# Seven stacked passes for the rest rows of the contraction, with their weights built ahead

## The chip, the cores and the metric

The kernel runs on one core of one Trainium2 chip. The metric is the device time of one execution in microseconds (us). The core has a matrix engine (PE, which loads a stationary tile of up to 128 x 128 and streams columns against it), a vector engine (DVE), a scalar engine (ACT), a general engine (POOL), and a queue (SP) from which this kernel issues all its DMAs. Each engine and the queue work off their own instructions strictly in the order of the program and wait for each other by semaphores.

## The reference

```
x  = A_x                                    # 1 x 2048 x 576
xn = layernorm(x)
out = x + A(xn) + B(xn)

A: qkv = xn @ wqkv                          # 576 x 1728, 32 heads of 18
   each token attends to 8 earlier tokens, 2 apart (0, 2, ..., 14 back), masked below token 0
   softmax over the 8, weighted sum of v, then @ wo           # 576 x 576
B: h = xn @ w1 + b1                         # 576 x 4608
   mish(h) = h * tanh(softplus(h)), then @ w2                 # 4608 x 576
```

All inputs and the output are fp32.

## The kernel before

**Number format.** A product of two fp32 matrices is made of three passes on PE in a rounded fp32 format: each operand is split into a high part (a cast, done by ACT) and a low part (what is left, a subtraction on DVE or POOL), and high x high, low x high and high x low are summed in PSUM.

**Halves, blocks, tiles.** The 2048 tokens are two halves (`hf`) of 1024. A half has two blocks (`b`) of 512 tokens, a block four tiles (`jj`) of 128. `ln_norm` or `norm1` normalises a tile, `ln_transpose` and `transpose_split` transpose it on PE and split it into the operand `XTs[hf, b]`.

**Seven products for eight.** The first 512 rows of the contraction and the 1024 tokens are cut in 2 x 2 blocks, the weights likewise, and a Strassen-Winograd scheme is used: with A11, A12, A21, A22 the token blocks by rows of the contraction, and B11 to B22 the weights (two feature tiles of F1, or two groups of QKV), the operands S1 to S4 and T1 to T4 are sums of them, and seven products (A11 B11, A12 B21, S1 T1, S2 T2, S3 T3, S4 B22, A22 T4) replace eight. A product of 256 rows is six passes (`prod`, line 986; in the QKV groups `za_part`, line 702). S is made once for a half (`s_step`, `s_high`, `s_low`, lines 943 to 981, the sums on POOL). T is made for each pair of F1 by `w1_sums` (POOL) and for the QKV groups by `za_sum` (DVE).

**The rest rows.** 576 = 512 + 64. The last 64 rows of the weights are held twice in a tile of 128 partitions, and the operand has the high part of the 64 rows above and the low part below. Two passes (`rest`, line 1000) with the weights' high and low part make a full product. The rest is not part of the seven products: four of them (A12 B21, S1 T1, A22 T4, S4 B22) get a rest product added, with the rest of block 0 or 1 or their difference (`rem`), so that the four outputs are whole. The rest weights are part of the tiles of F1's weights (`wa` is 5 x 128 wide, `wc` 3 x 128) and two units of their own (R2, R3) of a QKV group pair.

**The stages.** Half 0: the QKV groups 0 and 1 directly (`qkv_item`, 14 passes a tile, four tiles a block), the groups 2 and 3 by seven products ("y"), then 18 pairs `q` of F1's feature tiles (`m1_part`, parts 0 to 5), each followed by the second layer F2 for the pair before (`m2_pair`). The weights are loaded, split on ACT and DVE (`make`, `low`) and stored in DRAM in both parts (`keep`). Half 1: transposes between the last items of F2, then the groups 0 and 1 ("v") and 2 and 3 ("z") by seven products, then the 18 pairs with the kept weights (`fetch`), F2 by seven products for six pairs of pairs (`p_item`), and last the product with wo (`wo_part`). Attention runs beside F1: POOL multiplies, DVE sums; it reads k and v through four `kv` tiles (`load_kv`).

**The order.** `plan` is a list of items, each a piece of work on PE in that place, with background work that is issued just before it. `before(i, ...)` puts a load, a sum, a split or a store at item i; a table `MOVED` shifts some of them. Items 0 to 3 are group 0 of block 0 of half 0; 4 to 6 and 8 group 1 of block 0; 7, 9, 11 and 13 the transposes of the four tiles of block 1; 10, 12, 14 and 15 group 0 of block 1; 16 to 19 group 1 of block 1; "y" begins at item 20, attention's first step is at item 26. The raw weights of "y" are loaded at items 8 to 12 (`za_load`). PSUM has four banks with the tag `h` and four with the tag `out`; a transposed tile takes two of `h`, a QKV item one.

The steps of the prediction touch `transpose_split` (lines 317 to 339), `ln_norm` (440), `ln_transpose` (449), `qkv_item` (610), `first_item` (1543), `prod` and `rest` (986, 1000), `m1_part` (1057), `za_part` (702), `attention` (837) and the places in `plan` from line 1663 on.

## Time and profile before

| what | value |
|---|---|
| runs (3) | 1089.81, 1089.99, 1090.22 us, median 1089.99 |
| span of the profiled execution, first to last instruction | 1088.0 us (its own device time is not listed; the median run is 1.99 us longer than this span) |
| PE busy | 1081.0 us, 6454 matmuls |
| weight loads of PE | 997.7 us |
| DVE busy | 892.9 us, 1475 instructions |
| ACT busy | 513.6 us, 946 |
| POOL busy | 787.4 us, 630 |
| DMA | 283.99 MB, mean 261 GB/s |

The profile is of one execution. A row of the groups by line gives the line, the engine, the operation, the output and inputs by the program's names with their shapes, the count, then the busy time of the group and the mean of one instruction in ns, then the idle time ahead of them and who ended it. The chain of waits follows the work that ended last back to the start; its rows are start, length, engine and line. Matmuls overlap in the pipeline, so the length of one in the groups is more than what it adds to a row of them.

### The profile page before, as it was taken

To read this page: it belongs to the slowest core of one execution; us is meant where nothing else is said; L and a number is where in the kernel's file an instruction comes from. 1 tells how busy PE (TensorE), PEld (TensorE's weight loads), DVE (VectorE), ACT (ScalarE), POOL (GpSimd) and SP (SyncE) were. 2 spreads that over 40 slices of the span, in tenths; PEclk is the share of its full clock that TensorE was granted. 3 is DMA by queue.
4 is the path that set the end of the run, shared out by engine and by line. 5 is a ranking of instruction groups with operands and counts; after the bars stand their busy time and mean duration, and the time that the engine had idled before them with its cause. 6 is when DMAs were issued, how large, how long until landed. Compare 5 with 4: busy or idle time off the path is not lost.

```text
span 1088.0 us, 18205 instructions
## 1 busy us (share of the span) xinstructions
PE 1081.0 (99%) x6454; PEld 997.7 (92%) x6454; DVE 892.9 (82%) x1475; ACT 513.6 (47%) x946; POOL 787.4 (72%) x630
## 2 busy tenths in 40 slices
...
PEclk9999999999999999999999999999999999999999
...
GB/s 225 282 254 360 363 320 281 218 277 275 240 296 234 248 235 299 297 252 210 265 309 328 327 309 346 274 228 222 191 239 247 225 218 188 215 302 242 243 220 137
DMA packets 187327, 283.99 MB, mean 261 GB/s; under 512 B 53826, under 2 KB 127844, under 8 KB 187236
## 3 DMA queue, kind: packets, MB, share of 16 engines
...
## 4 chain that ended last, share of the span: by engine, by line
PE 92%; DMA 3%; DVE 2%; POOL 1%; SPq 1%; ACT 1%; issue 0%; POOLq 0%; ACTq 0%
PE h L995 30%; PE po L1101 20%; PE po L1193 12%; PE po L1215 7%; PE h L1001 6%; PE o L1398 5%; PE pq L628 3%; PE v L742 2%; PE y L742 2%; PE vT L742 1%; PE yT L742 1%; POOL pv L896 1%; SPq L932 1%; DMA kv<-kv_d 1%; DMA kv_d<-kvs_v 1%; DMA wa<-kept_wa 1%
## 5 line engine op out<-in xcount | busy, mean ns | idle before, releaser
L1101 PEld LDWEIGHTS po<-w,act 128*128 128x128 f32 x1728 | 236.2, 188 | 5.4
L1101 PE MATMUL po<-w,act 128*128 128x288 f32 x1728 | 240.7, 295 | 0.0
L896 POOL TENSOR_TENSOR pv<-L,kv 128x576 f32<-128x576 f32 x128 | 173.6, 1466 | 40.6 <-DVE L L889 35.7
L857 POOL TENSOR_TENSOR pr<-q,kv 128x576 f32<-128x576 f32 x128 | 195.8, 1566 | 3.3 <-DMA q<-q_d 3.0
L1051 POOL TENSOR_TENSOR act<-c,act 128x512 fp32r<-128x512 f32 x66 | 90.6, 1372 | 81.9 <-ACT act L1049 73.8
L1193 PEld LDWEIGHTS po<-pw,u 128*128 128x128 f32 x1008 | 137.9, 188 | 3.5 <-DVE u L1147 0.2
L1193 PE MATMUL po<-pw,u 128*128 128x288 f32 x1008 | 140.3, 295 | 0.0
L1105 DVE TENSOR_TENSOR acc<-po,acc 128x288 f32<-128x288 f32 x288 | 118.1, 448 | 22.7 <-PE po L1101 21.5
L995 PE MATMUL h<-S,t 128*128 128x512 f32 x432 | 110.4, 391 | 0.0
L995 PE MATMUL h<-xt,t 128*128 128x512 f32 x432 | 110.3, 390 | 0.0
L902 DVE TENSOR_REDUCE og<-pv 128x144 f32<-128x1152 f32 x64 | 86.2, 1348 | 24.0 <-POOL pv L896 23.9
L995 PE MATMUL h<-xt,wa 128*128 128x512 f32 x432 | 103.9, 389 | 0.1
L1044 ACT ACTIVATE c<-c,b1c 128x512 f32<-128x512 f32 x69 | 50.0, 724 | 100.9 <-DVE c L1043 100.8
L995 PEld LDWEIGHTS h<-xt,wa 128*128 128x128 f32 x432 | 80.8, 188 | 16.9 <-DMA wa<-kept_wa 0.5
L862 DVE TENSOR_REDUCE L<-pr 128x64 f32<-128x1152 f32 x64 | 85.5, 1342 | 12.1 <-POOL pr L857 12.1
L995 PEld LDWEIGHTS h<-xt,t 128*128 128x128 f32 x432 | 79.1, 188 | 14.5 <-DVE rt L1043 0.2
L995 PEld LDWEIGHTS h<-S,t 128*128 128x128 f32 x432 | 77.9, 188 | 13.4 <-ACT rm L1032 0.4
L1032 ACT COPY c<-h 128x512 f32<-128x512 f32 x68 | 39.8, 586 | 86.8 <-PE h L1001 43.8
L1215 PEld LDWEIGHTS po<-w,act 128*128 128x128 f32 x576 | 78.4, 188 | 1.6
L1215 PE MATMUL po<-w,act 128*128 128x288 f32 x576 | 79.5, 294 | 0.0
L1199 DVE TENSOR_TENSOR accP<-po,accP 128x288 f32<-128x288 f32 x156 | 63.0, 448 | 10.4 <-PE po L1193 7.5
L1043 DVE TENSOR_TENSOR c<-h,c 128x512 f32<-128x512 f32 x69 | 47.1, 683 | 26.9 <-PE h L1001 20.8
...
## 6 DMA issues: line engine op xcount, KB each, us to landing
kv<-kv_d SPq DMA_DIRECT2D x64, 396.0 KB, 6.4
...
```

The costliest lines, as they stand in the source:

```text
L742: nc.tensor.matmul(h, l, r_, start=i == 0 and name in ("B11", "B21", "T3"), stop=i == len(seq) - 1, skip_group_check=True)
L857: nc.gpsimd.tensor_tensor(out=pr[:, x:x + hh], in0=q[:, j0 + x:j0 + x + hh, None, :].to_broadcast([P, hh, W, CU]), in1=win(kt, 0, CU, j0 + ...
L862: nc.vector.tensor_reduce(L[:, k, j0:j0 + hj].rearrange("p j w h -> p (j w h)"), pr.rearrange("p j w (h d) -> p (j w h) d", h=2), axis=AX, ...
L896: nc.gpsimd.tensor_tensor(out=pr[:, x:x + hj].rearrange("p j d w -> p j w d"), in0=L[:, k, x:x + hj, :, h:h + 1].to_broadcast([P, hj, W, DH]),
L902: nc.vector.tensor_reduce(og[:, c0:c0 + DH, :].rearrange("p d j -> p j d"), pr, axis=AX, op=ALU.add)
L995: nc.tensor.matmul(ph, wt[:, wl, wk * P:(wk + 1) * P], X[:, xs, :], start=first and i == 0, stop=last and i == len(seq) - 1, skip_group_ch ...
L1001: nc.tensor.matmul(ph, wt[:, wl, off * P:(off + 1) * P], X[:, xs, :], start=False, stop=wl == 1, skip_group_check=True)
L1051: eng.tensor_tensor(out=a[:, 1, :], in0=t, in1=a[:, 0, :].bitcast(F32), op=ALU.subtract)
L1101: nc.tensor.matmul(po, acts[hf, q, b, j][:, al, tok], done["w2", hf, 2 * q + j][:, wl, c * HC:(c + 1) * HC], start=i == 0, stop=i == 5)
L1105: nc.vector.tensor_tensor(out=t, in0=po, in1=t, op=ALU.add)
L1193: nc.tensor.matmul(po, units[e, k, qq][:, al, tok], w[:, qq, wl, :], start=i == 0, stop=i == 5)
L1215: nc.tensor.matmul(po, acts[hf, q, b, j][:, al, tok], done["w2", hf, 2 * q + j][:, wl, c * HC:(c + 1) * HC], start=i == 0, stop=i == 5)
```

## The change

Now all seven products get a rest part, of one pass each. The 64 rest rows are cut into two pieces of 32 rows, and the seven-product scheme is used on these too: the piece of an operand (32 rows) is laid four times over the 128 partitions, its high part on some and its low part on the others, and the weights' high and low parts are laid against it, so that one pass of 128 rows sums the three partial products (and the low x low one). The plain QKV items use the same operands: two passes as before, one for each piece.

- `rest_dup` (ACT) copies a tile's 64 rest columns four times each into 256, two transposes bring them to PSUM (before one, two in block 1), and `rest_split` makes the operands: in block 0 A11 and A12; in block 1 A22, (in half 0) A21 and S1 to S4, whose sums are a reduction and a subtraction on DVE and two subtractions on POOL. It is called by `transpose_split` behind the split of the 512 rows; the split of S1 to S4 stands one item later on ACT, two later on DVE.
- The seven weights' rest pieces of all 18 pairs and of the QKV group pairs are built ahead, in seven chunks ("y", "v", "0" to "4"): load the four blocks, three T sums and a fourth on POOL (`c_sum`), high part on ACT (`c_high`), low part on DVE (`c_low`), store both parts in DRAM in pieces of 32 partitions (`c_keep`). This is at items 3 to 16. `wr_fetch` and `rest_fetch` bring the pieces back for each pair and each group pair by two DMAs of 64 partitions.
- For the plain groups the pieces are made by `rest_make` from a weight tile that is loaded fourfold, with a sign column, on ACT and DVE. The first item's two rest passes come only after the second item's other passes (`hold_open`).
- The weight tiles of F1 lose their rest columns (`wa` 4 x 128, `wc` 2 x 128), the units R2 and R3 are gone. Buffers are laid out anew: `kv` three instead of four, `tt` one double tile instead of two, `wc` now holds rest pieces, F1's `wc` has a buffer of its own, `pr` holds chunks and rest weights until attention begins. v's two loads of a pair of heads come one step apart, and so do the next k's. The rest rows of wo are kept as they were, loaded through other buffers.

```
-    def transpose_split(src, dst, col, extra=None, pair=False, both=None):
+    def transpose_split(src, dst, col, place, pair=False, both=None):
...
-        nc.tensor.transpose(tb[:, 0:P], src[:, KT * P:(KT + 1) * P], ident)
-        if extra is not None:
-            nc.tensor.transpose(tb[:, P:2 * P], extra, ident)
+        for k in range(2):
+            nc.tensor.transpose(tb[:, k * P:(k + 1) * P],
+                                rd[place[0], place[1] * JB + place[2]][:, k * P:(k + 1) * P], ident)
...
-        e = 1 if extra is None else 2
-        hr = dst[:, KT:KT + 5 * e - 4:5, col:col + P]
-        tbv = tb.rearrange("p (k t) -> p k t", k=KT)[:, 0:e]
-        nc.scalar.copy(hr, tbv)
-        nc.vector.tensor_sub(hr[64:P], tbv[64:P], hr[64:P].bitcast(F32))
+        rest_split(*place, tb.rearrange("p (k t) -> p k t", k=KT)[:, 0:2])
...
+    def rest_split(hf, b, jj, tbv):
+        X = XTs[hf, b]
+        at_ = slice(jj * P, (jj + 1) * P)
+        def split(dst, src):
+            nc.scalar.copy(dst, src)
+            return lambda: nc.vector.tensor_sub(dst[64:P], src[64:P], dst[64:P].bitcast(F32))
+        if b == 0:
+            low_ = split(X[:, 8:10, at_], tbv)
+            nc.scalar.copy(rr[hf][:, :, at_], tbv)
+            low_()
+            return
+        lows = [split(X[:, 8, at_], tbv[:, 1])]
+        if not hf:
+            lows.append(split(a21t[0][:, at_], tbv[:, 0]))
+        ss = sb.tile([P, 4, P], F32, tag="wd1", bufs=1, name=f"ss_{hf}_{jj}")
+        nc.vector.tensor_reduce(ss[:, 0], tbv.rearrange("p k t -> p t k"), axis=AX, op=ALU.add)
+        nc.vector.tensor_tensor(out=ss[:, 1], in0=rr[hf][:, 0, at_], in1=tbv[:, 0], op=ALU.subtract)
+        for low_ in lows:
+            low_()
+        nc.gpsimd.tensor_tensor(out=ss[:, 2], in0=ss[:, 0], in1=rr[hf][:, 0, at_], op=ALU.subtract)
+        nc.gpsimd.tensor_tensor(out=ss[:, 3], in0=rr[hf][:, 1, at_], in1=ss[:, 2], op=ALU.subtract)
+        last_ = []
+        plan[now[0] + 1][1].append(lambda: last_.append(split(X[:, 9:13, at_], ss)))
+        plan[now[0] + 2][1].insert(0, lambda: last_[0]())
...
+    def rest_dup(hf, n):
+        t = rd[hf, n] = sb.tile([P, 2 * P], F32, tag=("q", "wd0")[hf], bufs=(2, 1)[hf], name=f"rd_{hf}_{n}")
+        nc.scalar.copy(t.rearrange("p (k c d) -> p k c d", k=2, c=4), ...)
...
+    def rest_make(g, src):
+        t = done["wq", 0, g * 5 + 4] = new("wq", 0, g * 5 + 4)
+        nc.scalar.activation(t, src, AF.Identity, scale=sg[:, 0:1])
+        return lambda: nc.vector.scalar_tensor_tensor(out=t, in0=src, scalar=sg[:, 1:2], in1=t.bitcast(F32),
+                                                      op0=ALU.mult, op1=ALU.subtract)
...
+    def c_load(c):
+        n, w, rows = (7, QC, P) if c in "yv" else (7, P, P if c != "4" else 64)
+        tag = {"0": "S0", "1": "S1", "2": "S2", "3": "pr", "4": "pr", "y": "kv", "v": "kv"}[c]
...
+        nc.sync.dma_start(lo[:, 0:4], src)
+    def c_sum(c):
+        lo = chunk[c][0]
+        for o, a, b in ((4, 3, 0), (3, 2, 3), (5, 2, 4), (6, 1, 5)):
+            nc.gpsimd.tensor_tensor(out=lo[:, o], in0=lo[:, a], in1=lo[:, b], op=ALU.subtract)
+    def c_high(c):
+        nc.scalar.copy(chunk[c][1], chunk[c][0])
+    def c_low(c):
+        lo, hi = chunk[c]
+        nc.vector.tensor_tensor(out=lo.bitcast(F32R), in0=lo, in1=hi.bitcast(F32), op=ALU.subtract)
+    def c_keep(c):
...
+                for k in range(m):
+                    nc.sync.dma_start(ckept[c][k, h], t[k * RB:(k + 1) * RB].rearrange("p n w -> p (n w)"))
+    def wr_fetch(hf, q):
+        w = Q1[q] if hf else q
+        t = done["wr", hf, q] = sb.tile([P, 7, P], F32R, tag="wc", bufs=2, name=f"wr_{hf}_{q}")
+        src = ckept[str(w // CP)][w % CP].rearrange("h r n -> (h r) n")
+        for k in range(2):
+            nc.sync.dma_start(t[k * 64:(k + 1) * 64].rearrange("p n w -> p (n w)").bitcast(F32), src)
...
-                    if k == 0:
-                        vs.append(load_kv(hf, pair * PU + c, 1))
+                    if c == 1:
+                        vs.append(load_kv(hf, pair * PU + k, 1))
...
-                    if k == 0 and (pair + 1) * PU + h < NQ * UQ:
+                    if k == h and (pair + 1) * PU + h < NQ * UQ:
...
-    def prod(ph, wt, off, X, hi, lo, first, last, some=range(6)):
+    def prod(ph, wt, off, X, hi, lo, first, rest, some=range(7)):
+        seq = [(wt[:, wl, (off + k) * P:(off + k + 1) * P], X[:, xs + k, :])
+               for k in range(2) for wl, xs in ((0, hi), (0, lo), (1, hi))]
+        seq.append(rest)
...
+    for c, load_, sum_ in (("y", 3, 5), ("0", 3, 5), ("1", 4, 7), ("2", 4, 7), ("3", 6, 8), ("v", 9, 11), ("4", 11, 13)):
+        put(load_, lambda c=c: c_load(c))
+        put(sum_, lambda c=c: c_sum(c))
+        put(sum_ + 1, lambda c=c: c_high(c))
+        put(sum_ + 2, lambda c=c: c_low(c))
+        put(sum_ + 3, lambda c=c: c_keep(c))
+    for which, i in (("y", z0), ("v", v0), ("z", at["z", 0, 0])):
+        for n, d in enumerate((-4, -2, 4, 9)):
+            put(i + d, lambda which=which, n=n: rest_fetch(which, n))
+    for q in range(NP):
+        put(spot(0, q - 1, 2) if q > 1 else z0 + (11, 12)[q], lambda q=q: wr_fetch(0, q))
+        put(spot(1, q - 1, 2) if q > 1 else at["z", 0, 0] + (10, 12)[q], lambda q=q: wr_fetch(1, q))
+    for b in range(NB):
+        for jj in range(JB):
+            put(at["t", 1, b, jj] - 1, lambda n=b * JB + jj: rest_dup(1, n))
```

439 lines of the change are left out of this document (240 added, 199 removed).

## The prediction

> **What bounds the kernel now.** I read the page first: busy time by engine and the row of the granted clock.
>
> ```profile
> span 1088.0 us, 18205 instructions
> ...
> PE 1081.0 (99%) x6454; PEld 997.7 (92%) x6454; DVE 892.9 (82%) x1475; ACT 513.6 (47%) x946; POOL 787.4 (72%) x630
> ...
> PEclk9999999999999999999999999999999999999999
> ```
>
> Then the waits of the matmul engine, which say what ended each of its idle stretches.
>
> ```profile
> PE ta L325 <- ACT xn L444: 1.6, 2, 1.3
> PE warm L315 <- POOL ident masks.py:199: 1.3, 1, 1.3
> PE pq L628 <- ACT xt L331: 0.6, 1, 0.6
> PE pq L628 <- POOL wq L1520: 0.3, 1, 0.3
> ```
>
> TensorE (PE) is busy for 99% of the span, its clock is at full speed in every slice, and all its waits add up to 3.8 us, all in the first 18 us. So a column that PE does not stream shortens the run, unless something else becomes late. "Busy" alone would not prove that PE works at its rate, so I took the cost of one pass from the chain of waits in order of time (start, length, what), where runs of equal matmuls stand back to back:
>
> ```profile
> 58.62 4.69 PE y L742 x24
> ...
> 109.25 2.72 PE h L995 x12
> ```
>
> 24 passes of 432 columns take 4.69 us, 0.195 us each; 12 passes of 512 columns take 2.72 us, 0.227 us each. The groups by line give means of 358 and 389 ns for the same instructions, but those overlap; the chain's figure is what one pass is worth.
>
> **The passes that go.** The products of the 64 rest rows stand in groups of their own:
>
> ```profile
> L1001 PE MATMUL h<-xt,wc 128*128 128x512 f32 x144 | 44.4, 389 | 0.0
> L1001 PE MATMUL h<-xt,wa 128*128 128x512 f32 x144 | 44.3, 389 | 0.0
> ...
> L742 PE MATMUL y<-yw_R,xt 128*128 128x432 f32 x16 | 4.4, 358 | 0.0
> ```
>
> In F1 a pair of feature tiles in one half has four rest products of two passes, 288 passes over 36 pairs; seven stacked passes make 252. That removes 36 x 0.227 = 8.2 us. In a group pair of QKV, 32 rest passes (16 of them in the last row above) become 28; with three group pairs 12 x 0.195 = 2.3 us go. The plain QKV items keep 14 passes. Sum: 10.5 us less. I know of no reason in these rows for another price: the new pass has the same 128 rows and the same columns.
>
> **Transposes.** The rest block is now transposed twice for every tile, before it was once for the eight tiles of block 0. That is eight more, priced by the chain between tiles:
>
> ```profile
> 31.47 0.11 PE tb L326
> 31.58 0.11 PE tb L328
> ```
>
> 8 x 0.11 = +0.9 us (at least +0.5, since four of them come early, where PE waits anyway).
>
> **Start-up.** Up to 18 us one chain runs through statistics, normalisation and transposes, so what it gains in length PE waits for. Its last steps, from the timeline, are the root for tile 3 and that tile's transpose:
>
> ```profile
> 14.65 0.15 DVE L422 TENSOR_SCALAR ve<-mv 128x1 f32<-128x1 f32 x1
> ...
> 17.28 0.66 PE L325 MATMUL ta<-ident,xn 128*128 128x128 f32 x4 [0.31 <-ACT xn L444]
> ```
>
> Into it come a copy of 256 columns on ScalarE (ACT) behind each normalisation (rest_dup), and, between the statistics of tile 3 and its root, the low part of the stacked rest weights, 864 columns on VectorE (DVE). Their nearest rows:
>
> ```profile
> L338 ACT CAST xt<-tb 128x256 fp32r<-128x256 f32 x8 | 3.1, 387 | 0.0
> ```
>
> ```profile
> L538 DVE TENSOR_TENSOR wq<-rwq,wq 128x432 fp32r<-128x432 f32 x5 | 2.8, 604 | 1.6 <-ACT wq L537 1.6
> ...
> L334 DVE TENSOR_REDUCE s<-ta 128x256 f32<-128x512 f32 x8 | 5.4, 679 | 0.0
> ...
> L339 DVE TENSOR_TENSOR xt<-tb,xt 64x256 fp32r<-64x256 f32 x8 | 3.4, 428 | 0.2
> ```
>
> The copy is 0.39 us, the low part 2 x 0.604 = 1.2 us, together 1.6 us. ACT makes the high part first: by columns 864/256 x 0.387 = 1.3 us, and DVE may wait for all of it, so the upper end is 2.9 us. A cast of a fifth weight tile leaves ACT and pulls the other way; the lower end is 0.4 us. I take +1.7 us.
>
> **Transposed tiles of half 0 (20 to 50 us).** Here the seven chunks of rest weights are also built. The stretches of the trace (us, then busy time of PE, its loads, DVE, ACT, POOL, then clock and DMA):
>
> ```profile
> 20.00:30.00 10.00, 10.00 (x53) 9.56 (x52) 6.94 (x25) 5.09 (x15) 0.24 (x1) 1.00 0.78 274
> 30.00:40.00 10.00, 10.00 (x60) 9.36 (x59) 5.22 (x14) 6.07 (x17) 1.78 (x5) 1.00 1.03 373
> 40.00:50.00 10.00, 10.00 (x55) 9.54 (x54) 7.31 (x11) 4.98 (x14) 6.15 (x6) 1.00 0.69 224
> 50.00:75.00 25.00, 25.00 (x129) 23.89 (x129) 24.95 (x30) 14.28 (x37) 19.28 (x13) 1.00 0.64 218
> ...
> 500.00:550.00 50.00, 49.90 (x328) 47.52 (x328) 43.87 (x79) 26.45 (x54) 37.36 (x35) 1.00 0.66 224
> ```
>
> DVE has 30 - 6.94 - 5.22 - 7.31 = 10.5 us free between 20 and 50. By columns a chunk's low part is 1.1 us (756 columns, two chunks) or 1.25 us (896, five): 8.4 us. Each tile of block 1 gets half of a reduction of 0.68 (0.34), a subtraction (at most 0.43), two half-height lows (0.43 together) and a low of four times their width (0.86), less the 0.43 of now: 1.6 us, 6.4 us for four. That is 14.8 us into 10.5 us; the rest runs into 50 to 75, where DVE has nothing free. How soon PE feels it is seen at tile 0 of block 1: DVE's last read of the tile's banks, and PE's next item, which needs one of them:
>
> ```profile
> 34.53 0.43 DVE L339 TENSOR_TENSOR xt<-tb,xt 64x256 fp32r<-64x256 f32 x1
> ```
>
> ```profile
> 35.01 3.04 PE L628 MATMUL pq<-wq,xt 128*128 128x432 f32 x14
> ...
> 41.88 16.74 PE L628 MATMUL pq<-wq,xt 128*128 128x432 f32 x84
> ...
> 69.42 4.91 PE L742 MATMUL y<-yw_T,S 128*128 128x432 f32 x24
> ```
>
> 34.53 + 0.43 = 34.96, and PE goes on at 35.01: there is no margin. The reads of one tile grow by a reduction and a subtraction, 0.34 + 0.43 = 0.8 us; four tiles make 3.1 us. I take +3.0 us. The lower end is 0 (DVE's free time lies ahead of each tile), the upper 5 us (all the excess). Later the margin is wider. The low part that the third product of the "y" group needs:
>
> ```profile
> 66.79 3.83 DVE L690 TENSOR_TENSOR yw_T<-yT,yw_T 128x432 fp32r<-128x432 f32 x3
> ```
>
> The first of these three ends at about 68.1, and PE comes to its second half at about 70.5 (start 69.42 plus five passes), so 2.4 us are there, and the rest weight's own split of 1.7 us leaves DVE ahead of it. ACT's high parts, by columns from 0.387 us for 256, are 9.1 us, into 30 - 5.09 - 6.07 - 4.98 = 13.9 us free: nothing by itself. POOL's 28 subtractions of 128 columns go into its idle time:
>
> ```profile
> L458 POOL TENSOR_TENSOR rem<-rem,xn 128x128 f32<-128x128 f32 x4 | 1.8, 463 | 0.2
> ```
>
> 28 x 0.46 = 13 us, with 0.24 and 1.78 us busy of the twenty before 40: also nothing, as long as their data is there.
>
> The lows have two operands in SBUF, and such a DVE instruction is not always 0.604 us. In the window from 45 to 70, where POOL computes too, it is:
>
> ```profile
> L690 DVE TENSOR_TENSOR yw_T<-yT,yw_T 128x432 fp32r<-128x432 f32 x3 | 5.0, 1696 | 0.0
> ```
>
> [...] If every chunk met that, 8.4 us would be 23 us; if none, the sum above holds.
>
> **The chunks' stores and loads.** The new stores (52 in all, 32 partitions each) and loads are issued by one queue, SP's, and 40 stores stand between the loads of the y weights and the last two chunks. SP's queue in the stretch (start, length):
>
> ```profile
> 24.35 9.55 SPq L556 DMA_DIRECT2D kept_wq<-wq  x9
> ...
> 39.74 2.66 SPq L671 DMA_DIRECT2D yB<-in_wq  x5
> 48.09 0.38 SPq L638 DMA_DIRECT2D kv_d<-kvs  x1
> 48.56 0.53 SPq L643 DMA_DIRECT2D q_d<-qs  x1
> 59.08 0.36 SPq L638 DMA_DIRECT2D kv_d<-kvs  x1
> ```
>
> Between 42.4 and 59.1 it issues four DMAs. Their pitch is 48.56 - 48.09 = 0.47 us, so 40 stores are 19 us. Nearest by shape are the attention's stores, from 32 partitions too (ns, least/median/most):
>
> ```profile
> L932 SPq DMA_DIRECT2D o_d<-oT x72: 318/509/2722, 158.2 to 1029.0; - x72
> ```
>
> 0.32 to 0.51 us, so 13 to 20 us. I take a residue of +0.5 us for what comes late, at the lower end 0; the upper end is the rival below.
>
> **Half 1 (505 to 540 us).** The same four tiles: 6.4 us more for DVE, against 50 - 43.87 = 6.1 us free in that stretch. I take +0.7 us, ends 0 and 3.
>
> **The rest of the run.** Rest weights come by two DMAs per pair into a buffer of two, and attention has three instead of four kv tiles, each loaded a step later. What hides them is the step of attention (72 steps in about 520 us, 7 us each) against
>
> ```profile
> kv<-kv_d SPq DMA_DIRECT2D x64, 396.0 KB, 6.4
> ```
>
> 6.4 us to landing; the tile is wanted two steps on. 0, at the upper end +1 us, where a rest tile of the first two pairs lands late.
>
> **Sum**: -10.5 + 0.9 + 1.7 + 3.0 + 0.5 + 0.7 = -3.7 us, from a span of 1088.0 to 1084.3 us. The median of the runs is 1089.99, 1.99 us more than that span; with the same around it, **1086.3 us**. Own range of this case: 1083.5 to 1088.
>
> **Rivals.** (1) All extra work finds a hole: only the passes, 0.9 and half of the start-up remain, -10.5 + 0.9 + 0.9 = -8.7 us, **1081.3 us**. For it: PE's waits show that other engines were never late after 18 us. Against: the missing margin at 35 us.
>
> (2) The chunks arrive late and ACT stands in front of PE: **slower**. POOL sums chunk v behind its load, ACT casts it in item 12, ahead of the cast of tile 3, without which item 15 cannot run. SP issues 8 kept stores at 1.06 us (9.55/9), three chunk loads, two weight loads and 16 chunk stores before it gets there: from 26 (24.35 and the start-up), 8.5 + 2 + 2 + 8 + 2 (two sends, a load, its own) = 22.5, so 48.5 us. Its way to landing is bounded by the y weights' loads:
>
> ```profile
> DMA to landing us min/median/max: 6.1/6.1/6.1
> ```
>
> Between half of that and all of it: 51.5 to 54.6 us, plus 4 x 0.46 on POOL, a cast of 1.1 and about 2 us of other ACT work: 56.5 to 59.5 us, where PE wants tile 3 at 41.9 + 2.8 (14 of the 84 passes) + 4.7 = 49.4. Chunk 4 waits for 24 stores more, 12 us, and for the last of them to land; PE has four banks, so three items or 8.4 us, before it stops again. Together 6 to 13 us, 9.5 in the middle: 1086.3 + 9.5 = **1096 us**. It decides from the point where chunk v lands later than 49.4 - 5 = 44 us; with chunk stores at 0.32 us and the kept stores at the pitch of 0.47 instead of 1.06 (5 + 3 us sooner) it lands about there. Against it: the queue is nearly empty there now, and its pace of 1.06 was that of a full DMA. [...]
>
> (3) Gain and cost meet: start-up 2.9, tiles 5, half 1 3 and the rest 1 give -10.5 + 0.9 + 11.9 = +2.3 us at the very end; half way from the forecast to there is **1089.3 us**.
>
> (4) The passes don't shrink in number or each costs more: then the matmul count (6454 - 48 + 8 = 6414) shows it. I give it no chance of its own.
>
> **Numbers.** Forecast 0.32, (1) 0.15, (3) 0.15, (2) 0.30, and 0.08 for a late wait elsewhere that costs over 5 us. A measurement of this kernel tells about 0.2%, 2.2 us, from no change. Faster by more: 0.32 + 0.15 = 0.47; within: 0.15; slower: 0.30 + 0.08 = 0.38. The range reaches from just below (1) to above (2): 1080.5 to 1098.
>
> **What would show it.** Right: 6414 matmuls, passes at 0.227 and 0.195 us, transpose of tile 3 near 19 us, the first y product near 64 us instead of 58.6, and no PE wait after 90 us. Wrong: PE waits of several us on ACT between 40 and 65 us, with ACT itself behind a POOL subtraction and that behind a chunk's load (rival 2); a first y product before 61 us (rival 1); PE idle around 545 us.

## The result and the profile after

The changed kernel takes **1175.01 us** (median of four runs, 1174.44 to 1175.33) against 1090.07 us for the kernel before on the same chip: a ratio of **1.0779** (95% interval 1.0764 to 1.0794). It is slower by 85 us, where the forecast was a gain of 3.7 us and the range ended at 1098 us.

The page of the changed kernel, with busy time by engine and the row of the granted clock:

```profile
span 1173.3 us, 18469 instructions
...
PE 1099.6 (94%) x6414; PEld 1004.1 (86%) x6414; DVE 908.4 (77%) x1505; ACT 525.3 (45%) x975; POOL 798.2 (68%) x649
...
PEclk9887899999999999999989889999999999999999
```

PE was idle for 1173.3 - 1099.6 = 73.7 us, before for 1088.0 - 1081.0 = 7.0 us. That is 66.7 us more. Its busy time also grew, by 18.6 us, although 40 matmuls went away. By the prices of the prediction (10.5 us of passes less, 0.9 us of transposes more) it should have fallen by 9.6 us. So some 28.2 us of the busy time are passes that ran slower, and the row of the clock says where: in the same two places in which PE was idle. 66.7 + 28.2 - 9.6 = 85.3 us, the whole difference of the spans. On average a wait is paid for 1.4 times ((66.7 + 28.2) / 66.7).

The two places, in stretches of the trace (start and end, length, then busy time of PE, its loads, DVE, ACT, POOL, then clock, DMA share, GB/s). Before:

```profile
60.00:100.00 40.00, 40.00 (x201) 37.53 (x201) 36.54 (x54) 19.49 (x49) 27.30 (x20) 1.00 0.98 326
...
600.00:650.00 50.00, 49.95 (x245) 43.22 (x244) 35.78 (x53) 22.03 (x40) 36.72 (x29) 1.00 0.98 311
```

After:

```profile
20.00:60.00 40.00, 32.50 (x154) 28.59 (x153) 27.95 (x62) 24.80 (x63) 16.43 (x30) 0.91 0.79 260
60.00:100.00 40.00, 25.65 (x100) 22.68 (x100) 28.78 (x29) 13.73 (x37) 24.78 (x20) 0.74 0.75 217
...
200.00:500.00 300.00, 299.74 (x1819) 274.85 (x1819) 261.80 (x417) 150.84 (x247) 230.46 (x193) 1.00 0.80 266
...
600.00:650.00 50.00, 40.16 (x194) 37.46 (x194) 30.89 (x55) 12.71 (x39) 31.09 (x25) 0.93 0.84 232
650.00:700.00 50.00, 31.48 (x138) 28.27 (x137) 24.61 (x40) 6.23 (x20) 31.47 (x25) 0.80 0.87 267
```

In the long middle nothing is lost: 299.74 of 300 us at full clock. The waits of PE after, each with total, count and longest in us:

```profile
PE zT L791 <- DMA rest_z<-ckept_y: 9.8, 1, 9.8
PE z L791 <- DMA rest_z<-ckept_y: 8.7, 1, 8.7
PE h L1106 <- DMA wr<-ckept: 7.8, 2, 5.6
PE vT L791 <- DMA rest_v<-ckept_v: 7.8, 1, 7.8
PE y L791 <- DVE yw_B L744: 6.0, 2, 4.9
PE pq L670 <- ACT qs L678: 5.1, 1, 5.1
```

The three longest single waits are in half 1, on the rest pieces that come back from DRAM. The longer wait for `wr`, 5.6 us, is in half 0, in the first pair of F1 (it ends at 142.1 us); the other is 2.2 us, in half 1. The last two rows are between 20 and 100 us.

What a wait of PE does beyond its own length is seen on its timeline after (start, length, work, and in brackets the idle time ahead of it):

```profile
604.01 1.33 PE L791 MATMUL vT<-vw_T,xt 128*128 128x432 f32 x6
613.12 0.70 PE L791 MATMUL vT<-rest_v,xt 128*128 128x432 f32 x1 [7.79 <-DMA rest_v<-ckept_v]
613.62 2.36 PE L791 MATMUL vT<-vw_T,xt 128*128 128x432 f32 x6
...
617.79 1.33 PE L791 MATMUL vT<-vw_T,xt 128*128 128x432 f32 x6
```

Six passes that take 1.33 us take 2.36 us right after the wait of 7.79 us, and 1.33 us again four microseconds later. The granted clock was 0.50 of full speed from 613.1 to 616.1 us, 0.82 from there to 617.8 and 1.00 from 617.8 to 622.0; in the three microseconds behind the waits of 9.8 and 8.7 us (664.4 to 667.4, 691.5 to 694.5) it was 0.50 too. Of the waits above, 9.8, 8.7 and 7.8 us were followed by 1.7, 2.0 and 1.7 us of such loss (what the next passes took over their usual length). Some gaps of 2.2 us were followed by it as well (last section). The prediction left this out.

### The profile page after: what moved, and what is told of

Read it like the earlier page. It is cut to its first block, busy times and chain, and to the rows that moved or that the text cites. A ratio compares the mean times of both kernels' runs of the same rounds, so it can differ in the third digit from the quotient of the medians.

```text
span 1173.3 us, 18469 instructions
## 1 busy us (share of the span) xinstructions
PE 1099.6 (94%) x6414; PEld 1004.1 (86%) x6414; DVE 908.4 (77%) x1505; ACT 525.3 (45%) x975; POOL 798.2 (68%) x649
## 4 chain that ended last, share of the span: by engine, by line
PE 74%; DMA 6%; DVE 6%; POOL 5%; SPq 4%; issue 3%; ACT 2%; POOLq 0%; DVEq 0%; ACTq 0%
PE h L1106 30%; PE po L1203 15%; PE po L1295 10%; PE po L1317 6%; PE o L1482 5%; PE y L791 2%; DMA wr<-ckept 2%; POOL pv L1006 1%; PE vT L791 1%; PE zT L791 1%; POOL pr L967 1%; DMA rest_z<-ckept_y 1%; PE yT L791 1%; DMA ckept<-ck 1%; DMA z_T<-kept_yT 1%
## 5 line engine op out<-in xcount | busy, mean ns | idle before, releaser
L1006 POOL TENSOR_TENSOR pv<-L,kv 128x576 f32<-128x576 f32 x128 | 173.0, 1445 | 57.7 <-DVE L L999 23.1
L1106 PE MATMUL h<-xt,wa 128*128 128x512 f32 x432 | 111.6, 394 | 0.0
L1106 PE MATMUL h<-xt,wr 128*128 128x512 f32 x252 | 99.1, 393 | 7.8 <-DMA wr<-ckept 7.8
L1149 ACT ACTIVATE c<-c,cb 128x512 f32<-128x512 f32 x69 | 50.0, 724 | 101.9 <-DVE c L1148 101.9
L972 DVE TENSOR_REDUCE L<-pr 128x64 f32<-128x1152 f32 x64 | 85.6, 1341 | 10.5 <-POOL pr L967 10.3
L1106 PEld LDWEIGHTS h<-S,t 128*128 128x128 f32 x432 | 79.0, 190 | 13.7 <-ACT rm L1137 0.4
```

What stands on the lines that cost most here:

```text
L972: nc.vector.tensor_reduce(L[:, k, j0:j0 + hj].rearrange("p j w h -> p (j w h)"), pr.rearrange("p j w (h d) -> p (j w h) d", h=2), axis=AX, ...
L1006: nc.gpsimd.tensor_tensor(out=pr[:, x:x + hj].rearrange("p j d w -> p j w d"), in0=L[:, k, x:x + hj, :, h:h + 1].to_broadcast([P, hj, W, DH]),
L1106: nc.tensor.matmul(ph, l, r_, start=first and i == 0, stop=i == len(seq) - 1, skip_group_check=True)
```

## The experiments

All columns but the last three are marks on PE's timeline in the profiled execution, as us later than before: the first "y" product (before at 58.5), the first pair of F1 (94.6), the first transposes of half 1 (506.6), "v" (536.6), "z" (576.2), F1 in half 1 (612.3), F2 in half 1 (643.6). Then the span, the median of the runs, and the ratio to the kernel before on the same chip with its 95% interval.

| kernel | y | F1 | t | v | z | F1 | F2 | span | median | ratio |
|---|---|---|---|---|---|---|---|---|---|---|
| changed | +22.1 | +40.4 | +46.0 | +48.2 | +60.7 | +82.3 | +86.1 | +85.3 | 1175.01 | 1.0764–1.0794 |
| e1 | +21.2 | +34.6 | +41.2 | +43.4 | +55.7 | +74.2 | +77.1 | +76.6 | 1168.32 | 1.0697–1.0733 |
| e2 | +9.6 | +23.1 | +29.1 | +31.3 | +43.4 | +65.0 | +67.5 | +66.2 | 1155.62 | 1.0576–1.0608 |
| e3 | +15.9 | +28.6 | +34.8 | +37.0 | +49.4 | +71.2 | +75.7 | +75.1 | 1164.88 | 1.0663–1.0695 |
| e4 | +46.7 | +64.9 | +70.2 | +72.3 | +84.7 | +105.6 | +110.3 | +109.9 | 1199.56 | 1.0975–1.1019 |
| e5 | +21.4 | +38.3 | +36.4 | +38.6 | +46.6 | +59.2 | +66.7 | +66.0 | 1154.43 | 1.0565–1.0607 |
| e6 | +5.5 | +15.1 | +14.0 | +16.2 | +26.9 | +34.3 | +45.3 | +44.7 | 1135.14 | 1.0392–1.0435 |
| e7 | +4.3 | +14.3 | +12.6 | +14.8 | +26.2 | +34.2 | +40.0 | +39.0 | 1130.74 | 1.0359–1.0395 |
| e8 | +31.1 | +31.3 | +31.3 | +31.3 | +31.3 | +31.3 | +30.8 | +31.1 | 1120.15 | 1.0256–1.0291 |
| e9 | 0.0 | 0.0 | +1.0 | +1.0 | +6.1 | +8.8 | +13.7 | +13.8 | 1104.51 | 1.0123–1.0159 |
| e10 | +4.2 | +10.5 | +8.6 | +10.8 | +21.7 | +30.3 | +36.1 | +35.6 | 1128.31 | 1.0329–1.0382 |
| e11 | +3.5 | +10.3 | +9.3 | +10.3 | +14.6 | +23.7 | +32.7 | +32.5 | 1123.44 | 1.0295–1.0332 |
| e12 | +3.6 | +8.4 | +7.1 | +8.2 | +12.6 | +21.7 | +31.3 | +30.6 | 1117.31 | 1.0235–1.0278 |
| e13 | +4.1 | +8.0 | +6.2 | +7.2 | +11.3 | +18.8 | +25.2 | +24.7 | 1115.69 | 1.0221–1.0252 |
| e14 | +21.4 | +39.6 | +44.8 | +45.8 | +56.7 | +71.0 | +72.3 | +71.3 | 1161.33 | 1.0636–1.0668 |
| e15 | +20.7 | +35.3 | +33.5 | +34.6 | +39.0 | +47.8 | +52.1 | +51.5 | 1142.82 | 1.0473–1.0508 |
| e16 | +3.5 | +8.5 | +6.6 | +7.7 | +12.5 | +12.4 | +21.0 | +20.1 | 1110.11 | 1.0167–1.0198 |
| e17 | +13.4 | +35.0 | +41.0 | +43.2 | +55.5 | +77.1 | +81.5 | +81.0 | 1168.22 | 1.0677–1.0739 |
| e18 | +14.5 | +29.9 | +28.5 | +30.7 | +38.6 | +48.7 | +59.9 | +59.3 | 1147.64 | 1.0497–1.0537 |

### The chunks in half 0

**e3**: chunk "4", the last of the seven, is not built; the pieces of its pairs are those of chunk "3".

```
-        src = ckept[str(w // CP)][w % CP]...
+        src = ckept[str(min(w // CP, 3))][w % CP]...
-    for c, load_, sum_ in ((...), ("v", 9, 11), ("4", 11, 13)):
+    for c, load_, sum_ in ((...), ("v", 9, 11)):
```

> Left out: the building of chunk 4 alone (pairs 16 and 17 read chunk 3's pieces). Theory A: POOL's wait of 12.3 us for this chunk's load holds the S sums, ACT's cast (11.8 us) and through it PE (5.1 us) and the y weights' splits (3.2 and 4.9 us); 10 to 20 us less, 1155 to 1165. Rival C (the number of stores in SP's queue is what counts): only four of 52 stores and one load go, 2 to 3 us, 1172 to 1175.

It came out 10.1 us faster than the changed kernel (1164.88 against 1175.01), and PE's wait of 5.1 us for `qs` is gone. In the changed kernel the path to that wait can be read through four timelines. SP's queue (start, length, count):

```profile
52.33 8.77 SPq L895 DMA_DIRECT2D ckept<-ck  x16
...
61.67 3.70 SPq L895 DMA_DIRECT2D ckept<-ck  x8
66.15 0.56 SPq L868 DMA_DIRECT2D ck<-in_w1r  x1
```

The load of chunk 4 goes out at 66.15, behind 24 stores. POOL:

```profile
68.94 1.91 POOL L873 TENSOR_TENSOR ck<-ck 64x128 f32<-64x128 f32 x4 [12.31 <-DMA ck<-in_w1r]
...
71.75 2.96 POOL L1059 TENSOR_TENSOR s<-s,xt 128x512 f32<-128x512 f32 x2
```

It stood for 12.31 us at the chunk's sums, with the last tile's subtraction and the S sums of the seven products behind it. ACT:

```profile
70.88 0.94 ACT L876 CAST ck<-ck 64x896 fp32r<-64x896 f32 x1 [11.78 <-DMA ckept_v<-ck_v]
...
72.35 0.39 ACT L677 COPY kvs<-pq 128x288 f32<-128x288 f32 x1
```

And PE:

```profile
72.98 4.63 PE L670 MATMUL pq<-wq,xt 128*128 128x432 f32 x12 [5.10 <-ACT qs L678]
```

ACT's cast of chunk 4 stands in front of the copies that empty PE's banks. The row names a DMA as what ended the cast's wait, but the cast starts at 70.88 us, when POOL's sums of the chunk end (68.94 + 1.91 = 70.85). This is the mechanism of rival 2, and it is worth 10 us of 85. PE's 12 passes behind it take 4.63 instead of 2.52 us.

**e2**: only the chunks "y" and "0" are built, and all pieces are read from these two.

```
-        src = ckept[str(w // CP)][w % CP]...
+        src = ckept["0"][w % CP]...
-        c = "y" if which in "yz" else "v"
+        c = "y"
-    for c, load_, sum_ in (("y", 3, 5), ("0", 3, 5), ("1", 4, 7), ...):
+    for c, load_, sum_ in (("y", 3, 5), ("0", 3, 5)):
```

> Left out: the building of the chunks v, 1, 2, 3 and 4; every pair reads the pieces of chunk 0 and all QKV groups those of chunk y, so passes and fetches are the same in number and size. Theory A: what comes late between 35 and 110 us is the chunks' doing (queue, POOL, ACT); the second F1 pair begins 35 to 47 us sooner than at 156 us, total 1128 to 1140; the waits in half 1 stay. Rival B (the transposed tiles' own added splits of S1 to S4 on DVE and ACT hold PE): half or more of the early loss stays, 1150 to 1170.

19.4 us faster; the first y product is 9.6 us late instead of 22.1. So five of the seven chunks, chunk 4 among them, cost 19 us, while from "v" to F2 this kernel loses 36.2 us, about as much as the changed kernel (37.9).

**e4**: each half chunk is stored by one DMA of 128 partitions instead of four of 32, with the four pieces as DRAM's outermost dimension.

```
-                for k in range(CP):
-                    nc.sync.dma_start(ckept[c][h, :, k], t[k * RB:(k + 1) * RB]...)
+                nc.sync.dma_start(bass.AP(..., ap=[[7 * QC, CP], [CP * 7 * QC, RB], [1, 7 * QC]]), t...)
```

> Edit: each part of a chunk is stored by one DMA of its 128 partitions instead of four of 32, into the same places (14 stores, before 52, same bytes). Rival C (issue time of the stores, about 0.5 us each, delays the y weights and chunk 4): 38 x 0.5 = 19 us of queue go, the y weights and chunk 4 land 10 to 19 us sooner and 10 to 20 us of the early loss goes, 1155 to 1165. If the bytes or the landing count (chunk 4 waits for chunk 3's stores to land, POOL for chunk 4): under 5 us, 1170 to 1175.

24.5 us **slower**. The stretches of this kernel (columns as above):

```profile
81.00:86.00 5.00, 0.00 (x0) 0.00 (x0) 0.00 (x0) 0.00 (x0) 0.00 (x0) 0.83 0.26 104
86.00:91.00 5.00, 0.00 (x0) 0.00 (x0) 0.00 (x0) 0.00 (x0) 0.00 (x0) 0.50 0.33 124
```

Every engine stands for the ten microseconds, and in the first five the DMA engines are busy for 0.26 of their time, at 104 GB/s; four of sixteen would be 0.25. The outermost dimension of these stores is four. That four engines did the work is an estimate from this share; no view shows it engine by engine. And SP's queue of the same kernel shows that what comes next pays for it:

```profile
41.05 4.32 SPq L895 DMA_DIRECT2D ckept<-ck  x2
45.47 3.51 SPq L691 DMA_DIRECT2D kv_d<-kvs  x1
49.07 9.39 SPq L696 DMA_DIRECT2D q_d<-qs  x1
```

Two small stores, 0.38 and 0.57 us in the changed kernel, take 3.51 and 9.39 us to issue, though ACT had written their data by 43.84 us.

**e17**: the same wide stores, but with the 32 rows as the outermost dimension; the weights are laid out in that order.

```
+                nc.sync.dma_start(ckept[c][h].rearrange("r k n -> (r k) n"), t...)
...
+                nc.sync.dma_start(bass.AP(..., ap=[[7 * P, RB], [2 * RB * 7 * P, m], [1, 7 * P]]), t...)
```

> As the wide stores (1199.6): one store of 128 partitions for each part of a chunk, but the rows of a chunk are laid out so that the outermost of a store's places in DRAM counts 32 or 128 and not four. If the wide stores were slow because four outermost places are worked by four of the sixteen DMA engines (share 0.26 in that run between 76 and 86 us): the queue no longer stands at them, total 1155 to 1172, below the changed kernel's 1175. If it is the store's size: 1190 to 1200 again.

1168.22 us: 31.3 us faster than e4 and 6.8 us faster than the changed kernel. SP's queue of e17, to set beside 8.77 us for 16 stores:

```profile
48.74 3.34 SPq L894 DMA_DIRECT2D ckept<-ck  x4
```

So the 40 narrow stores, 20.3 us of queue time in the changed kernel (4.20 + 3.65 + 8.77 + 3.70), cost at most some 6.8 us more than wide ones. In e17 the DMA engines are full between 36 and 56 us (shares 1.03 and 1.08), so that the bytes themselves may be what is left; no run shows that.

**e8**: the kernel before, with the seven chunks built at the same items and read by nobody.

```
+    for c, load_, sum_ in (("y", 3, 5), ("0", 3, 5), ("1", 4, 7), ("2", 4, 7), ("3", 6, 8), ("v", 9, 11), ("4", 11, 13)):
+        plan_put(load_, lambda c=c: c_load(c))
...
+        plan_put(sum_ + 3, lambda c=c: c_keep(c))
```

> The kernel before, with one part of the change added: the seven chunks are loaded, summed, split and stored at the same items as in the changed kernel, and nobody reads them. Theory A (building at this place costs by itself: ACT's casts and DVE's low parts stand in front of the tiles, chunk 4 holds POOL): 1110 to 1135, with PE waits between 35 and 90 us. Rival (building fits into the free time and only collides with the new splits of the transposed tiles): 1090 to 1098.

1120.15 us, 30 us slower than before, and all of it is lost ahead of the first y product (+31.1). Its waits of PE, then POOL's timeline:

```profile
PE tb L331 <- POOL rem L461: 24.2, 4, 10.7
```

```profile
55.23 1.76 POOL L850 TENSOR_TENSOR ck_v<-ck_v 128x108 f32<-128x108 f32 x4 [9.76 <-DMA ck_v<-in_wqr]
56.95 0.45 POOL L461 TENSOR_TENSOR rem<-rem,xn 128x128 f32<-128x128 f32 x1
```

POOL's sums of a chunk wait for its load, and behind them stands the difference that the next transpose needs. The victim is another than in the changed kernel, but the cause is of the same kind: a sum put on an engine at a fixed place in its order, ahead of data that its own load has not brought.

### Half 1 and the last piece

**e1**: "T1" and "T2" change places in the order of the products' weights, so that the parts of the first products come sooner.

```
-    CORDER = ("B11", "B21", "B22", "T3", "T1", "T2", "T4")
+    CORDER = ("B11", "B21", "B22", "T3", "T2", "T1", "T4")
-        for o, a, b in ((4, 3, 0), (3, 2, 3), (5, 2, 4), (6, 1, 5)):
+        for o, a, b in ((5, 3, 0), (3, 2, 3), (4, 2, 5), (6, 1, 4)):
-        ops_ = ((0, 1), (5, 6), (3, 4), (2,))[n]
+        ops_ = ((0, 1), (3, 4), (5, 6), (2,))[n]
```

> Edit: only the order in which the rest pieces of a QKV group pair share buffers: T2 with T3 and T1 with T4 (now T2 with T4 and T3 with T1), so that the third piece is wanted at the ninth item and not at the seventh, four items after its buffer comes free. Theory A (the loss is made of waits for late pieces and late chunks, and of slow passes behind each wait): the waits for the T3 piece in y (2.7 us), v (7.8) and z (9.8) go, with some 1 to 2 us of slow passes behind each; 20 to 27 us less than the changed kernel's 1175, so 1148 to 1155, and the stage before the first y product stays as it is. Rival B (DVE and ACT simply have too much to do): the work is the same, so 1172 to 1178.

6.7 us faster, a fraction of what was expected. The longest wait of PE in e1:

```profile
PE z L791 <- DMA rest_z<-ckept_y: 10.1, 1, 10.1
```

The waits of 9.8 us at `zT` and 7.8 us at `vT` have shrunk to 3.1 and 1.7 us, but the fourth piece of "z" now takes 10.1 us. The pieces pass through two buffers, and a wait that is taken from one piece stands at the next.

**e5**: e1, and the fourth piece is fetched as soon as its buffer is free (two items in, one for "z", instead of nine), the first pair's `wr` two or three items sooner.

```
-        for n, d in enumerate((-4, -2, 4, 9)):
+        for n, d in enumerate((-4, -2, 4, 1 if which == "z" else 2)):
-        put(... else z0 + (11, 12)[q], lambda q=q: wr_fetch(0, q))
+        put(... else z0 + (8, 12)[q], lambda q=q: wr_fetch(0, q))
```

> Edit: the order of the first experiment (T2 with T3, T1 with T4), and in addition the last rest piece of a QKV group pair is fetched eight items sooner for z and seven for y and v (its buffer is free), and the first F1 pair's pieces two to three items sooner. Theory A (a fetch is late because of the place it is issued from and because its buffer comes free too late): the waits for rest pieces of z (10.1 us left in the first experiment) and for wr (8.1) go with the slow passes behind them, 15 to 28 us less than that experiment's 1168, 1140 to 1153. Rival (SP's queue stands there anyway, behind attention's loads which wait for one of three kv tiles): the waits move to other pieces, 1160 to 1168.

20.6 us faster than the changed kernel. In two stages: between "v" and F2 e5 loses 28.1 us against before, the changed kernel 37.9; and from the first pair of F1 to the transposes of half 1 e5 gains 1.9 us, where the changed kernel, whose first pairs wait for `wr`, loses 5.6.

**e9**: the kernel before, with three `kv` tiles instead of four, the changed kernel's steps for the loads of k and v, and one of the first raw weights in another buffer because of it.

```
-        t = sb.tile([P, TJ + HALO, CU], F32, tag="kv", bufs=4, ...)
+        t = sb.tile([P, TJ + HALO, CU], F32, tag="kv", bufs=3, ...)
-                    if k == 0:
-                        vs.append(load_kv(hf, pair * PU + c, 1))
+                    if c == 1:
+                        vs.append(load_kv(hf, pair * PU + k, 1))
```

> The kernel before, with one part of the change: three kv tiles instead of four, attention's loads at the changed kernel's steps, and one of the first raw weights in another buffer because of it. Theory A (with three tiles a kv load waits in SP's queue for a free tile, 6 to 9 us in the v and z stages, and what stands behind it lands late): PE waits for v, z and F1 weights between 550 and 680 us, 1095 to 1110. Rival (the loads have room: my forecast counted them as nothing): 1089 to 1092.

1104.51 us, a ratio of 1.0141: **15 us slower** than before, and nearly all of it between 537 and 657 us. The waits of PE in e9:

```profile
PE h L995 <- DVE rt L1043: 3.5, 1, 3.5
PE v L742 <- DMA vw_T<-kept_vT: 3.5, 1, 3.5
```

SP's queue between 537 and 660 us, what its loads of `kv` wait for (total, count, longest), before and in e9:

```profile
SPq L812 <- POOL pv L896: 1.9, 1, 1.9
```

```profile
SPq L812 <- POOL pv L896: 9.8, 3, 6.7
```

Nothing here has to do with seven products or rest pieces. POOL's `pv` reads the `kv` tiles, and a load waits until it has freed one; with three tiles the queue stands 9.8 us at these loads instead of 1.9, and the weights behind them come late. POOL in turn waits 9.2 us for `kv` in this stretch, which it did not before. What the missing tile and the moved steps do one without the other was not run in this kernel.

### What is left without the chunks

**e6**: e5 without any building of chunks; the pieces are read from weights that are kept anyway, so that the bytes are fetched and the sums are not made.

```
-        src = ckept[str(w // CP)][w % CP].rearrange("h r n -> (h r) n")
+        src = kept["wq", q % 4].rearrange("(a b) n -> a (b n)", b=2)[:, 0:7 * P]
...
-    for c, load_, sum_ in (("y", 3, 5), ("0", 3, 5), ...):
-        put(load_, lambda c=c: c_load(c))
...
```

> Left out, beside the edits of the early fetches: all building of chunks; the pieces are read from a kept weight tile instead, in the same number of passes and fetches and the same bytes. What is left of the change is its passes, its start-up and the splits of its transposed tiles. Theory A (chunks and fetches make nearly all of the loss): second F1 pair at 109 to 118 us (before 109, changed kernel 156), total 1090 - 9 + 2 + 3 to 12 = 1086 to 1095. Rival B (the tiles' splits, with POOL's two subtractions standing between DVE and ACT in every tile, make a good part): first y product still some 8 us late and DVE behind in the y weights, total 1098 to 1115.

1135.14 us: 19.3 us less than e5, but still 45 us over the kernel before, where at most 1115 was expected. The first y product is 5.5 us late (the start-up is 2.3 of it), F1 15.1, and from "v" to F2 it loses 29.1 us. So the chunks, 19 of the 64 us that e5 loses, are not the main cause.

**e7**: e6, with the split of S1 to S4 in half 0 one item later on both engines, from a buffer of two.

```
-        ss = sb.tile([P, 4, P], F32, tag="wd1", bufs=1, ...)
+        ss = sb.tile([P, 4, P], F32, tag=("pr", "wd1")[hf], bufs=(2, 1)[hf], ...)
-        plan[now[0] + 1][1].append(lambda: last_.append(split(X[:, 9:13, at_], ss)))
+        plan[now[0] + (2, 1)[hf]][1].append(lambda: last_.append(split(X[:, 9:13, at_], ss)))
```

> The same without chunks, and the split of S1 to S4 of a tile in half 0 stands one item later on ACT and DVE, with two buffers instead of one for its sums, so that ACT no longer waits for POOL ahead of the copies that free PE's banks. Theory B (the loop tile - DVE sums - POOL sums - ACT split - copies sets a pitch of 4.3 us for each tile, and POOL's S sums stand behind the last tile): ACT's waits of 1.2 us for POOL go and the first y product comes 3 to 6 us sooner, total 4 to 10 us below the kernel without chunks. If that loop doesn't bind: the same within 1 us.

4.4 us less.

**e10**: e7, with POOL's two subtractions for the last two tiles three items later, and their split another item later.

```
+        if hf or jj < 2:
+            sums()
+        else:
+            plan[now[0] + 3][1].append(sums)
```

> As the kernel without chunks and with the later split of S1 to S4 (1130.7), and POOL's two subtractions for the last two tiles of block 1 stand three items later, behind the first S sums. Theory A (POOL works in order: its S sums stood at 50.6 instead of 41.0 us because the last tile's subtractions were ahead of them, and DVE's y work behind the S sums came late, PE's wait of 6.5 us for yw_B): S sums start near 43 us, that wait goes, first F1 pair at 100 to 103 us instead of 108.9, total 1121 to 1126. Rival (S sums wait for the transposed tiles' data, or DVE is simply full): within 2 us of 1130.7.

2.4 us less by the medians, with intervals that overlap, and 3.4 us by the spans. The start of the S sums on POOL, before, then in e7, then in e10:

```profile
41.00 2.66 POOL L950 TENSOR_TENSOR s<-s,xt 128x512 f32<-128x512 f32 x2
```

```profile
49.66 0.46 POOL L347 TENSOR_TENSOR ss<-ss,rr 128x128 f32<-128x128 f32 x1 [2.87 <-DVE ss L343]
...
50.62 3.46 POOL L1059 TENSOR_TENSOR s<-s,xt 128x512 f32<-128x512 f32 x2
```

```profile
42.84 3.11 POOL L1064 TENSOR_TENSOR s<-s,xt 128x512 f32<-128x512 f32 x2
```

In e7 they start 9.6 us later than before, behind the last tile's subtractions of 0.46 us each, which wait for DVE; in the changed kernel, at 71.75, behind chunk 4 as well. In e10 they start at 42.84 us, and F1 is 3.8 us less late.

**e11**: e7 with four `kv` tiles; S3 and S4 give up their room for it and are not split.

```
-    XR_OF = dict(A11=8, A12=9, A22=8, S1=9, S3=10, S2=11, S4=12)
+    XR_OF = dict(A11=8, A12=9, A22=8, S1=9, S3=10, S2=9, S4=10)
-        t = sb.tile([P, TJ + HALO, CU], F32, tag="kv", bufs=3, ...)
+        t = sb.tile([P, TJ + HALO, CU], F32, tag="kv", bufs=4, ...)
```

> As the kernel without chunks and with the later split of S1 to S4 (1130.7), and four kv tiles instead of three; room for it is made by leaving out the splits of S3 and S4 (their passes read S1 and S2: same passes, half the width in one cast and one low part for each tile). Theory A: kv loads no longer stand in SP's queue, the waits for vw_T (4.1 us), rest_z (2.8), wr (4.0) and qs_z (2.0) shrink with the slow passes behind them, total 1108 to 1120. Rival (the DMA engines are full there, share 1.0, and the stacked pieces add bytes): within 4 us of 1130.7.

7.3 us less than e7. By the marks the splits that are left out seem to have the larger part: F1 comes 4.0 us earlier and "t" to "v" is 1.2 us shorter, while from "v" to F2, where e9 loses by the missing tile, it is 2.8 us. The two parts of the edit were not run apart.

**e12**: e10 and e11 together.

```
 e10's edit and e11's edit
```

> Both edits together: later sums on POOL and four kv tiles, no chunks, late split. Theory A: the two losses are in different stages and add up, 1100 to 1114; if the passes' gain is to show at all, it must be here, near 1090. Rival: another wait takes over and the sum of the two gains is not reached by more than 5 us.

13.4 us less than e7, more than the two one by one (2.4 and 7.3). Its profiled run is the slowest of its four (1120.69 against the median of 1117.31), so its marks are some 3 us pessimistic.

**e13**: e12 with the loads of k and v at the steps of the kernel before.

```
-                    if c == 1:
-                        vs.append(load_kv(hf, pair * PU + k, 1))
+                    if k == 0:
+                        vs.append(load_kv(hf, pair * PU + c, 1))
```

> As the kernel without chunks and with later sums and four kv tiles (1117.3), and attention's loads of k and v at the steps of the kernel before (one step sooner). Theory A (in the v and z stages POOL waits 3.5 to 6.6 us for each kv load because it is issued a step later, so POOL falls behind, its buffers come free late, and the next kv load stands in SP's queue ahead of the rest pieces): POOL's waits for kv go, the waits for rest_z (4.5 us) and wr (7.2) shrink, the first F2 item of half 1 at 655 to 662 us instead of 674.8, total 1098 to 1106. Rival (the DMA engines are full in that stage and the pieces late for it): 1113 to 1119.

1.6 us less by the medians, with intervals that overlap. With four tiles the load steps are little of what half 1 loses by.

**e16**: e13, and the rest pieces of "z" are not fetched; its products read v's last piece.

```
+        if which == "z":
+            for o in ops_:
+                rcols[which, CORDER[o]] = rcols["v", "B22"]
+            return
```

> As the kernel without chunks and with old load steps (1115.7), and the rest pieces of z are not fetched (its passes read one of v's pieces): 1.5 MB less to move between 580 and 615 us, where the DMA engines' share is 1.05. Theory D (the DMA engines are full in the z stage, so the added bytes make pieces late, whatever the queue does): the wait for rest_z (5.4 us) and its slow passes go and wr lands sooner; from the first z product to the first F1 pair 36 to 38 us instead of 43.6, total 1104 to 1110. Rival (queue order alone): the wait moves to z's other weights, total 1112 to 1117.

1110.11 us, 5.6 us less than e13. From the first z product to F1 it takes 36.04 us, as before the change (36.12); e13 takes 43.60. The stretch in e13, then in e16:

```profile
600.00:620.00 20.00, 14.44 (x65) 13.11 (x66) 8.98 (x12) 4.65 (x16) 15.88 (x13) 0.84 1.08 349
```

```profile
600.00:620.00 20.00, 20.00 (x104) 19.24 (x103) 14.43 (x22) 4.65 (x16) 17.74 (x14) 1.00 1.05 377
```

In both the DMA engines have no room (shares of 1.08 and 1.05), but in e16 PE does not stand. So the fetches of the pieces of "z", 1.5 MB, are what this stage loses by, 7.6 us in this kernel; 2.2 us of that are lost again between F1 and F2. Whether a better order of the same loads would have been enough, no run tells. Then the first pairs still wait; in e16:

```profile
PE h L1115 <- DMA wr<-kept_wq: 6.5, 2, 4.0
PE v L796 <- DMA rest_v<-kept_wq: 2.2, 1, 2.2
```

### The changed kernel, with parts undone

**e14** is the changed kernel, **e15** e5, each with four `kv` tiles, the load steps of before, and S3 and S4 not split; these two leave out part of the work. **e18** is e5 with the stores of e17, with nothing left out.

```
e14, e15
-    XR_OF = dict(..., S1=9, S3=10, S2=11, S4=12)
+    XR_OF = dict(..., S1=9, S3=10, S2=9, S4=10)
-        t = sb.tile([P, TJ + HALO, CU], F32, tag="kv", bufs=3, ...)
+        t = sb.tile([P, TJ + HALO, CU], F32, tag="kv", bufs=4, ...)
-                    if c == 1:
-                        vs.append(load_kv(hf, pair * PU + k, 1))
+                    if k == 0:
+                        vs.append(load_kv(hf, pair * PU + c, 1))
e18
+                nc.sync.dma_start(ckept[c][h].rearrange("r k n -> (r k) n"), t...)
```

> The changed kernel itself with one part undone: four kv tiles and attention's loads at the steps of the kernel before; room is made by leaving out the splits of S3 and S4 (their passes read S1 and S2; half the width in one cast and one low part for each tile). Theory A (three kv tiles cost the old kernel 14.9 us alone and stand in front of the rest pieces here): half 1 loses 15 to 28 us less, total 1147 to 1160. Rival (the pieces' own places decide in this kernel): 1168 to 1175.

> The same undone part together with the early fetches (1154.4 with three tiles). Theory A: both causes of the half-1 loss are gone; from the first transposes of half 1 to the end no more than 8 us lost against the kernel before, total 1125 to 1138, and what is left is the early stage with the chunks. Rival: 1145 to 1154.

> The early fetches (1154.4) with these wide stores, a complete version of the change. If 38 store issues fewer bring the y weights and chunk 4 sooner: 1135 to 1150. If chunk building is held by POOL, ACT and DVE order: 1150 to 1155. Either way above 1090, since the kernel without any chunk is at 1135 with the same fetches.

1161.33, 1142.82 and 1147.64 us. e14 is 13.7 us under the changed kernel and e15 11.6 us under e5; from "v" to F2 it is 11.4 and 10.6 us. In the kernel before, the same stage lost 12.7 us to the missing tile and the moved steps (e9). SP's loads of `kv` wait 0.3 us for POOL's `pv` in e14 between 537 and 740 us, and 11.2 us in the changed kernel. e18 is the fastest form of the change that computes everything, 27 us better than the changed kernel and still 5.2% slower than before.

## Why the prediction was wrong

**Passes: right.** There are 6414 matmuls. A pair of F1 in the steady part, by the starts of one group of passes a pair apart, before:

```profile
205.41 2.88 PE L995 MATMUL h<-xt,wa 128*128 128x512 f32 x12
...
229.49 2.88 PE L995 MATMUL h<-xt,wa 128*128 128x512 f32 x12
```

After:

```profile
204.46 1.52 PE L1106 MATMUL h<-xt,wa 128*128 128x512 f32 x6
...
228.31 1.52 PE L1106 MATMUL h<-xt,wa 128*128 128x512 f32 x6
```

24.08 against 23.85 us: one pass less, 0.23 us, as priced at 0.227. Rivals 1 and 3 fall with the total, rival 4 with this.

**Start-up: nearly right.** Tile 3's transposes went from 17.28 to 19.62 us, +2.3 against +1.7, inside its ends of 0.4 and 2.9.

**Tiles and chunks of half 0: the price mis-sized, by the way of counting.** The prediction had the first y product near 64 us; it came at 80.6. It added up work by engine. Its +3.0 is 0.8 us of longer reads for each of four tiles, the excess of DVE's work over its free time (14.8 into 10.5 us, so 4.3) is only its upper end, put at 5, and +0.5 stands for late chunks. The work itself was counted nearly right: the seven chunks' low parts on DVE took 9.0 us, where 8.4 was counted and 23 was the case that each runs at the pace of 1696 ns and not of 604. Between 60 and 100 us DVE, ACT and POOL were all less busy than before. What was late was the order. DVE stood for 11.1 us until 72.5, waiting for ACT behind chunk 4's cast, and then had no room to catch up:

```profile
80.00:90.00 10.00, 2.70 (x9) 1.44 (x7) 10.00 (x9) 4.90 (x13) 8.54 (x7) 0.71 0.57 135
```

DVE is full while PE waits for the y weights that DVE splits (6.0 us). A tile's new operands go from DVE to POOL to ACT and back, and what waited on an engine held up what was behind it: POOL 12.31 us and ACT 11.78 us at chunk 4, and with no chunk POOL 2.87 us for DVE's sums ahead of the S sums (e7). Without any chunk this makes the first F1 pair 14 to 15 us late (e6, e7), where the prediction allowed 5 for the tiles and 2.9 for the start; the late S sums on POOL are 3.8 us of it (e10). The prediction did not follow the S sums at all.

**Rival 2: right in mechanism, but it is 10 us of 85** (e3). Its price of 6 to 13 us holds. Chunk v's load was issued at 50.1 us, where it had put 48.5, after its point of decision; but behind chunk v PE waited only 0.3 us for ACT and 0.8 for DVE, and the 5.1 us came with chunk 4. What it missed is that the other chunks it did not price cost a further 9 us (e2, 19.4 less 10.1, if the two add); by which waits was not taken apart. Between 42.4 and 59.1 us it counted four DMAs of SP, where its rows show three; nothing in its sum hangs on that. The 40 narrow stores took 20.3 us of queue time, where the prediction counted 19 by their pitch, and wide stores gained 6.8 us (e17).

**"The rest of the run": the step that failed.** It said 0, +1 at the upper end, because a load lands in 6.4 us, a step of attention lasts 7 us, and a tile is wanted two steps on. From the transposes of half 1 to F2 the changed kernel loses another 40 us, and the first pair of half 0 waits 5.6 us for `wr`. In the prediction's own list this is the late wait elsewhere, to which it gave 0.08 and no price. Two errors are in the step.

First, the cover of the `kv` loads was read from means over the run. In this stage the DMA engines were full before the change (the row 600 to 650 shows a share of 0.98), and what decides is when a tile comes free. e9, the kernel before with one `kv` tile fewer and the loads moved, costs 14.9 us by itself.

Second, the rest pieces were not followed item by item and in the order of the queue. The third piece is wanted two items after its buffer comes free, and it does not land by then; e1 gives it two items more, and its waits shrink. And it does not go out when its buffer is free. In the changed kernel the last pass on v's first piece, the longest wait of the queue in that stretch (601 to 609 us), then the same kind of wait ahead of the fourth piece of "z" (680 to 688 us) and the two loads after it:

```profile
596.84 0.36 PE L791 MATMUL vB<-rest_v,xt 128*128 128x432 f32 x1
```

```profile
SPq L691 <- DVE qs_v L796: 8.2, 1, 8.2
```

```profile
SPq L922 <- POOL pv L1006: 4.9, 1, 4.9
```

```profile
686.77 0.34 SPq L922 DMA_DIRECT2D kv<-kv_d  x1
687.15 1.18 SPq L911 DMA_DIRECT2D rest_z<-ckept_y  x2
```

In "v" the buffer is free at 597.2 us and the load goes out at 606.98, because SP stands 8.2 us at a store whose data DVE has not made; PE then waits 7.8 us. In "z" a `kv` load stands 4.9 us, until POOL's `pv` has freed a tile, and `rest_z`, for which PE waits 8.7 us until 691.6, goes out right behind it. The fetch of the fourth piece and of the first `wr` at a better place is worth 13.9 us by the medians (e5 against e1); by the marks 8.5 us are gained from the first pair of F1 to the transposes of half 1, and 5.6 us from "v" to F2. "No PE wait after 90 us" was the sign named for a right prediction; the four longest single waits stand after that.

**The clock: missing.** Some 28 of the 85 us are passes at a lower granted clock (0.50 in the three microseconds behind each of the three longest waits). No term had them, and they turned waits of 8.7 and 9.8 us into 10.7 and 11.5.

**Half-1 tiles: inside the ends.** +0.7 was forecast, between 0 and 3; from "t" to "v" the changed kernel takes 2.2 us longer than before, and so do the others with all four splits. Where S3 and S4 are not split it is 1.0 or 1.1 (e11 to e16).

**What stays open.** e16, without chunks, z's pieces and with four `kv` tiles, is still 20 us over before: 8.5 us by F1, of which 2.3 are the start-up, 4.8 us in "v" with waits on its pieces (2.2 and 1.6), and 8.6 us from F1 to F2 with 6.5 us of waits on `wr`. These are pieces that the scheme must fetch; a kernel in which they come in time was not found.
